# Five more slots for split operands, early splits of a down stage, and all attention units among the ups

## The chip, the cores and the metric

The kernel runs on one core of a Trainium2 chip. TensorE (PE in the profile) multiplies matrices into PSUM, VectorE (DVE), ScalarE (ACT) and GpSimd (POOL) work on tiles in SBUF and PSUM (POOL on SBUF alone), and SyncE (SP) issues the DMA transfers, in order, from one queue. The metric is the device time of one execution in microseconds.

## The reference

The reference is a banded attention followed by a gated feed-forward layer, in float32:

```
scores = q @ k^T / 8, for batch 8, 8 heads, 576 positions, head size 64
scores = where(0 <= i - j < 64, scores, -1e9)
p      = exp(scores - rowmax); p = p / (rowsum + 1e-9)
x      = (p @ v), heads side by side: 4608 tokens x 512
out    = (sigmoid(x @ w_gate) * (x @ w_val)) @ w_out      512 -> 1536 -> 512
```

The three weights arrive as float64 and are turned into float32 on the chip.

## The kernel before

**Precision.** A float32 operand that TensorE multiplies is split into a high part (a cast on ACT) and a low part (a subtraction on VectorE); a product of two operands is three matmuls, high x high, high x low and low x high (`three`). So each operand that streams through TensorE costs one ACT cast, one VectorE subtraction and a slot of 128 x 2 x 384 in SBUF.

**Stages.** Tokens are cut into 12 tiles of 384. The first two (s=0) go through a plain scheme while weights are converted. The rest go in five stages s = 1 to 5 of two tiles each. Each has an up part (the gate and value products, `product`) and a down part (the product with w_out). The up part of a stage, and the down parts from s=2 on, multiply 2 x 2 blocks with seven block products instead of eight (`PRODUCTS`, n = 0 to 6): operands are sums and differences of blocks, called B11, T1, T2, T3, T4, B21, B22, and the products are added up by `combine`. The down of s=1 is plain (`plain_down`, 24 operands in two halves each).

The ups run k = 0 to 5 (six slices of the hidden layer), and in each k the seven products n, for gate and value (m = 0, 1): 42 products of 12 matmuls. The schedule numbers them u = 7k + n. The downs from s=2 on run n = 0 to 6, and in each n the six k (`last_product`, 6 matmuls): 42 steps, called d.

**The operands.** The x operands of a stage's ups (`x_part`, `x_rest`) lie in 14 slots x0 to x13, two for each n. The operands of a down, `h_part` i = 6n + k, go into the same 14 slots in turn (`h_split`, line 702). A slot becomes free when the last k of the ups has used its x operand, so the first 14 down operands are made in the last sixth of the ups (k = 5) or just behind it, and part i > 13 when part i - 14 has been used. For T2 and T4, `rhs_of` first makes the difference on VectorE (lines 571, 573), in place of B11. Before these, `h_prep` makes T1 and T3 of a k (`differences`, lines 563 and 564), and `x_prep` does the same for x.

**PSUM.** Each of gate and value (m), or of the two halves of a down (q), has three banks, one for each sum b of the seven products (`acc[m][b]`): n = 0 and 4 go to b=0, n = 1, 3, 5 to b=1, n = 2 and 6 to b=2. Product n=3 adds onto n=1 in b=1 after VectorE has read it (`plus`, line 607), and so on; a product group waits until the readers of its bank are done. A result uses 384 of the 512 columns of a bank. Two more banks (tag a) serve attention.

**Attention units.** The attention of stage s+1 is cut into eight units (a tile and a pair of heads), run while stage s is multiplied. A unit goes through: `stage_s` (scores on TensorE, band mask and row minimum on VectorE, exponentials on ACT), `stage_n` (reciprocals of the sums on VectorE, multiplication by them on POOL, or on VectorE for s+1 = 2), `stage_b` (six transposes into PSUM, copied to pT by ACT, line 304) and the outputs pT x v. The outputs of a unit run at the start of `stage_s` of the next unit; they give three pieces of 128 columns. Two go into free columns of the two attention banks, the third into columns 384 to 511 of a bank of `acc`, found by `spare_up` (b=0, after its sum is done at n=5) or by `spare_down` (a bank of the down, taken early and marked as held). ACT copies the pieces to xf. The last unit's outputs run by themselves (`stage_c`). Exponentials and sigmoids use different tables of ACT, so each unit costs two table loads.

In the kernel before, `visit` puts a unit's scores at u = 5, 12, 19, 26, 33, 40 (units 1 to 6) and at d = 10 (unit 7); unit 0 is at u=0, or ahead of s=1. Transposes follow four products after the scores and three products before the next unit's outputs; those of unit 6 run at d=8, of unit 7 at d=18, and unit 7's outputs at d=22.

**What sets the order.** Each piece of work is put into a list with a time (`put`), the times coming from a count of TensorE's steps; the list is sorted and traced in that order. The tile framework then simulates the program and orders each engine's instructions by what is ready and by their place in the trace; TensorE's own order is kept as traced (`pe`). `tc.issue_after(ins)` holds an instruction behind `ins` in the order of `ins`'s engine, without a wait. On each engine and in SP's queue, what waits holds up all behind it.

**Weights.** `w_load` brings 512 KB of up weights for one k and n into one of seven slots W, `wo_load` 512 KB of down weights into one of seven slots wo. The first seven down weights of a stage are put 80 us ahead of its down. In the down of s=1, `wo_sums` makes the sums of w_out blocks and stores them to DRAM for later stages.

## Time and profile before

| | |
|---|---|
| three runs | 977.72, 980.62, 982.87 us; median 980.62 |
| profiled execution | 980.85 us, span of its instructions 979.0 us |
| ups of s=1, down of s=1 | 212.2 to 318.4, to 372.7 us |
| ups and down of s=2 | to 484.8, to 534.1 us |
| ups and down of s=3 | to 639.6, to 688.9 us |
| ups and down of s=4 | to 794.4, to 843.7 us |
| ups and down of s=5 | to 931.0 us, to the end |
| mean granted TensorE clock | 0.996 |

In a row of the timeline stand start, busy time, engine, line, operation, out<-in, shape and count; in square brackets the engine's idle time before the first of them and what ended it. Matmuls overlap in time, so the time that a group takes on TensorE is read from its start to the start of the next group: 12 matmuls of 384 columns show 2.2 to 2.4 us of busy time and follow each other every 2.08. Tiles: pr are up products, y down products, s and pp the two attention banks (scores, transposes), pT the transposed weights of attention; h operands of a down, wt up weights, wot down weights.

### The profile page before, as it was taken

The page shows a single profiled execution, that of the slowest core. Times are in us where ns is not written, and L with a number is a line of the kernel's source. Part 1 is how long each engine was busy: PE and PEld are TensorE (multiplying, and loading weights), DVE is VectorE, ACT ScalarE, POOL GpSimd, SP SyncE. Part 2 cuts the span into 40 slices and gives each one's busy share as a digit, 9 for nine tenths or more (in the row PEclk, how much of TensorE's full clock was granted, in tenths as well). Part 3 has the DMA queues.
Part 4 walks back from the last instruction along what each step waited for, and adds up shares of the span by engine and source line. Part 5 has one row for each costly group of instructions (what it writes and reads, how often), then busy time and mean ns, then how long its engine had stood idle before and what let it go on. Part 6 is the DMA issues. An engine that isn't in the chain of part 4 may idle for free.

```text
span 979.0 us, 20624 instructions
## 1 busy us (share of the span) xinstructions
PE 953.7 (97%) x7200; PEld 906.8 (93%) x7200; DVE 697.2 (71%) x1873; ACT 589.0 (60%) x1473; POOL 142.7 (15%) x232
## 2 busy tenths in 40 slices
PE   6899999999999998999999999999999999999998
PEld 5798999889989998999999999899999989999998
DVE  7889989656668756566877566797566697656783
ACT  7888878545757645555775555685555666412351
POOL 4201104227670000010010101010010100000000
PEclk9999999999999999899999999999999999999999
DMA  9899999948998778887779888879888876988465
GB/s 345 308 381 378 388 345 355 396 151 292 310 315 276 248 259 298 305 266 256 250 240 309 278 269 263 246 250 286 296 262 267 265 228 218 306 254 253 152 201 165
DMA packets 110839, 272.42 MB, mean 278 GB/s; under 512 B 12048, under 2 KB 42896, under 8 KB 110736
## 3 DMA queue, kind: packets, MB, share of 16 engines
q1 hardware_dynamic: 110736, 271.11, 83.0%
q8 instruction: 57, 0.93, 0.4%
q14 instruction: 46, 0.38, 0.1%
HBM read 214.17 MB, written 56.89 MB: 277 GB/s over the span
## 4 chain that ended last, share of the span: by engine, by line
PE 67%; DVE 12%; ACT 7%; DMA 5%; issue 3%; POOL 3%; SPq 1%; DVEq 0%; POOLq 0%; ACTq 0%
PE pr L597 31%; PE y L597 14%; PE ph L358 10%; PE y L414 5%; PE s L219 3%; ACT p L251 2%; DVE h L705 2%; DMA a<-w32d 2%; PE pp L299 2%; DMA wa<-w32d 2%; PE s L328 1%; POOL ws L550 1%; DVE h L571 1%; PE oo L328 1%; DVE h L640 1%
## 5 line engine op out<-in xcount | busy, mean ns | idle before, releaser
L597 PE MATMUL pr<-x_T,wt 128*128 128x384 f32 x1224 | 226.5, 336 | 4.4 <-DVE c L607 3.6
L597 PEld LDWEIGHTS pr<-x_T,wt 128*128 128x128 f32 x1224 | 211.8, 188 | 8.0 <-DVE c L607 5.9
L597 PE MATMUL pr<-x_B,wt 128*128 128x384 f32 x1008 | 189.6, 339 | 0.0
L597 PEld LDWEIGHTS pr<-x_B,wt 128*128 128x128 f32 x1008 | 176.8, 190 | 3.3 <-issue 2.9
L597 PE MATMUL y<-h,wot 128*128 128x384 f32 x1008 | 178.9, 336 | 0.3 <-DVE h L640 0.3
L597 PEld LDWEIGHTS y<-h,wot 128*128 128x128 f32 x1008 | 174.4, 188 | 1.4 <-DVE h L640 0.6
L268 POOL TENSOR_TENSOR p<-p,rs 128x384 f32<-128x384 f32 x76 | 67.1, 897 | 606.3 <-DVE rs L259 464.1
L367 ACT ACTIVATE g<-c 128x384 f32<-128x384 f32 x90 | 47.3, 525 | 129.9 <-DVE c L636 128.4
L251 ACT ACTIVATE p<-p,mn 128x128 f32<-128x128 f32 x288 | 111.1, 393 | 7.8 <-DVE mn L243 7.2
L704 ACT CAST h<-h 128x384 fp32r<-128x384 f32 x168 | 81.8, 513 | 52.1 <-PE y L597 30.8
L358 PE MATMUL ph<-x,w 128*128 128x384 f32 x576 | 106.1, 338 | 0.0
L705 DVE TENSOR_TENSOR h<-h,h 128x384 fp32r<-128x384 f32 x168 | 93.3, 584 | 17.9 <-ACT h L704 17.7
L358 PEld LDWEIGHTS ph<-x,w 128*128 128x128 f32 x576 | 99.7, 188 | 2.2 <-issue 0.9
L640 DVE TENSOR_TENSOR h<-c,g 128x384 f32<-128x384 f32 x90 | 54.9, 610 | 46.1 <-ACT g L367 40.7
L243 DVE CUSTOM_DVE_ANT_0 p<-s,m 128x128 f32<-128x128 f32 x288 | 65.6, 285 | 17.0 <-PE s L219 16.9
L304 ACT COPY pT<-pp 128x384 f32<-128x384 f32 x96 | 41.1, 481 | 36.2 <-PE pp L299 36.2
L607 DVE TENSOR_TENSOR c<-pr,p 128x384 f32<-128x384 f32 x60 | 33.1, 552 | 40.1 <-PE pr L597 40.1
L219 PE MATMUL s<-k,q 64*64 64x128 f32 x1152 | 47.3, 293 | 8.7 <-DMA k<-in_kT_dram 6.1
L367 ACT ACT_TABLE_LOAD x37 | 47.5, 1283 | 6.6 <-DMA out_dram<-yo 6.0
L251 ACT ACTIVATION_READ_ACCUMULATOR p<-p,mn 128x1 f32 x264 | 49.7, 188 | 0.0
L219 PEld LDWEIGHTS s<-k,q 64*64 64x64 f32 x1152 | 34.4, 141 | 15.5 <-DMA q<-in_qT_dram 5.0
L636 DVE TENSOR_TENSOR c<-pr,p 128x384 f32<-128x384 f32 x60 | 33.1, 555 | 20.3 <-PE pr L597 20.2
(115 smaller groups left out, 1338.3 us busy)
## 6 DMA issues: line engine op xcount, KB each, us to landing
wt<-wd SPq DMA_DIRECT2D x186, 512.0 KB, 4.5
wot<-wod SPq DMA_DIRECT2D x84, 512.0 KB, 4.5
v<-in_vN_dram SPq DMA_DIRECT2D x48, 384.0 KB, 5.1
wd<-ws SPq DMA_DIRECT2D x48, 256.0 KB, 4.9
k<-in_kT_dram SPq DMA_DIRECT2D x48, 224.0 KB, 5.0
q<-in_qT_dram SPq DMA_DIRECT2D x48, 192.0 KB, 5.0
w32d<-w SPq DMA_DIRECT2D x36, 256.0 KB, 5.4
wd<-w SPq DMA_DIRECT2D x36, 256.0 KB, 5.9
```

Of the source, the lines that this page charges most:

```text
L219: pe(nc.tensor.matmul(sc[h][half * BLK:(half + 1) * BLK, u, :], qt[h * BLK:(h + 1) * BLK, U * BLK:(U + 1) * BLK], kt[h * BLK:(h + 1) * BLK ...
L243: nc.vector.tensor_tensor_reduce(out=pt[:, u, :], in0=sc[:, u, :], in1=masks[key], op0=ALU.add, op1=ALU.min, scale=-SCALE, scalar=3.0e38, ...
L251: exp = nc.scalar.activation(pt[:, u, :], pt[:, u, :], AF.Exp, bias=mn[:, u:u + 1], scale=-1.0, **sums)
L268: eng.tensor_mul(out=pt, in0=pt, in1=rs.unsqueeze(2).broadcast_to([P, UP, P]))
L304: cp = nc.scalar.copy(pT, pp)
L358: pe(nc.tensor.matmul(ph, l, r, start=i == 0, stop=i == len(prs) - 1))
L367: act = nc.scalar.activation(g, c, AF.Sigmoid)
L414: pe(nc.tensor.matmul(yb[y], l, r, start=first and n == 0, stop=last and n == 2))
L597: pe(nc.tensor.matmul(ps, l, r, start=first and i == 0, stop=last and i == 2, skip_group_check=not check))
L640: nc.vector.tensor_mul(out=hidden(s, k)[2 * r + b], in0=c, in1=gates.pop((t, j)))
L704: nc.scalar.copy(h2[:, 0, :], src)
L705: nc.vector.tensor_sub(out=h2[:, 1, :], in0=src, in1=h2[:, 0, :].bitcast(F32))
```

## The change

- **Five slots more.** The buffer that the program reserves for DMA descriptors made on the chip shrinks to 1 KB, since every transfer here is issued by SP; in its room lie five more slots e0 to e4 of the split-operand size. `h_split` now goes around 19 slots, the five first.
- **First splits along with the ups.** For s > 1, `h_early` makes down operands 0 to 4 (n=0, k = 0 to 4) and the T2 differences of these k as soon as each k is done. Operand i is now reused for i + 19, and the due times of the other `h_part`s follow. `GUARD` holds operands 8 to 12 behind the latest `plus` on VectorE. In the plain down of s=1, the operands take the 19 slots too.
- **x operands earlier.** The slots become free earlier in a down, so `x_prep`, `x_part` and `x_rest` of the next stage are due four steps earlier (ten in the down of s=1). `x_prep` of s=2 is held behind the latest `plus`.
- **All attention units in the ups.** Scores now stand at u = 4, 9, 14, 19, 25, 30, 35 (`VISITS`), normalization at u+1, transposes at u+4, and the last outputs at u=41. So five of the six transposes that a next unit follows stand one product ahead of its outputs, and unit 0's (u=3, for s > 1) too. The third output piece goes into whichever bank fits: b=2 when n=4, b=0 otherwise, and where a sum is under way in that bank, the matmuls don't restart it. `spare_down` goes away.
- **Down weights of s=2** are due 48 us instead of 80 us ahead of their down, behind the latest `w_load` in SP's queue.

```diff
-    WB, WOB, CB = 7, 7, 3
+    WB, WOB, CB, EXTRA = 7, 7, 3, 5
...
-            oo = [sc[0][:, UP, :], sc[1][:, UP, :], spare()]
-            outputs(*done, oo)
+            piece, start = spare_up(spare)
+            oo = [sc[0][:, UP, :], sc[1][:, UP, :], piece]
+            outputs(*done, oo, (True, True, start))
...
-    def outputs(t, p, oo):
+    def outputs(t, p, oo, starts=(True,) * UP):
...
-                                    pT[h][:, U // 2, half * BLK:(half + 1) * BLK], start=True, stop=True))
+                                    pT[h][:, U // 2, half * BLK:(half + 1) * BLK],
+                                    start=starts[U // 2], stop=True, skip_group_check=not starts[U // 2]))
...
-        nc.sync.dma_start(out=w2.bitcast(F32), in_=wd[k][n])
+        marks["w_load"] = nc.sync.dma_start(out=w2.bitcast(F32), in_=wd[k][n]).ins
...
-        nc.sync.dma_start(out=w2.bitcast(F32), in_=wod[q])
+        with tc.issue_after(marks["w_load"]) if s == 2 else nullcontext():
+            nc.sync.dma_start(out=w2.bitcast(F32), in_=wod[q])
...
-        if nm == "T2":
+        if nm == "T2" and not any(src is x for x in t2_made):
...
+    t2_made = []
+    GUARD = (8, 13)
+
+    def h_early(s, k):
+        h_part(s, 0, k)
+        b11, _, _, b22, t1 = hidden(s, k)
+        nc.vector.tensor_sub(out=b11, in0=b22, in1=t1)
+        t2_made.append(hidden(s, k))
...
-        differences(nc.vector, b11, b12, b22, t1)
+        with tc.issue_after(marks["plus"]) if s == 2 else nullcontext():
+            differences(nc.vector, b11, b12, b22, t1)
...
-            nc.vector.tensor_add(out=o, in0=ps, in1=a)
+            marks["plus"] = nc.vector.tensor_add(out=o, in0=ps, in1=a).ins
...
-        h2 = xp.tile([P, 2, TT], F32R, name=f"h_{nm}", tag=f"x{i % (2 * NPR)}")
+        i %= EXTRA + 2 * NPR
+        h2 = xp.tile([P, 2, TT], F32R, name=f"h_{nm}", tag=f"e{i}" if i < EXTRA else f"x{i - EXTRA}")
...
-        hs[(s, n, k)] = h_split(f"{n}_{s}_{k}", n * NK + k, rhs_of(nc.vector, hidden(s, k), PRODUCTS[n][1]))
+        i = n * NK + k
+        with tc.issue_after(marks["plus"]) if GUARD[0] <= i < GUARD[1] else nullcontext():
+            hs[(s, n, k)] = h_split(f"{n}_{s}_{k}", i, rhs_of(nc.vector, hidden(s, k), PRODUCTS[n][1]))
...
-    def spare_up():
-        return acc[0][0][:, TT:TT + P]
-
-    def spare_down(s):
-        acc[0][2] = psum(1, 2, f"y2_0_{s}")
-        acc[0][("held", 2)] = True
-        return acc[0][2][:, TT:TT + P]
+    def spare_up(n):
+        return acc[0][2 if n == 4 else 0][:, TT:TT + P], n > 4
...
+    VISITS = (4, 9, 14, 19, 25, 30, 35)
...
-            for v in range(1, NP * 2 - 1):
-                visit(("u", NPR * v - 2), 3, *unit(s + 1, v), unit(s + 1, v - 1), spare_up)
-                visit(("u", NPR * v - 1), 4, *unit(s + 1, v))
-                visit(("u", NPR * v + 2) if v < 6 else ("d", 8), 1, *unit(s + 1, v))
-            visit(("d", 10), 3, *unit(s + 1, 7), unit(s + 1, 6), lambda s=s: spare_down(s))
-            visit(("d", 12), 4, *unit(s + 1, 7))
-            visit(("d", 18), 1, *unit(s + 1, 7))
-            visit(("d", 22), 2, *unit(s + 1, 7))
+            for v, u in enumerate(VISITS, 1):
+                visit(("u", u), 3, *unit(s + 1, v), unit(s + 1, v - 1), u % NPR)
+                visit(("u", u + 1), 4, *unit(s + 1, v))
+                visit(("u", u + 4), 1, *unit(s + 1, v))
+            visit(("u", 41), 2, *unit(s + 1, 7))
...
                 put(now + 0.5, 5, h_prep, s, k)
+                if k < EXTRA:
+                    put(now + 3, 5.1, h_early, s, k)
...
-                put(at_down[2 * i - 28] + 2.3 if i > 13 else t0 - 14.5 + 2.1 * (i // 2 + 1) if i < 10 else t0 - 1, 5.2,
-                    plain_part, i)
-            x_parts(at_down[24], lambda x: at_down[28 + 2 * x] + 2.4 if x < 10 else at_down[46] + 2.4 + 1.05 * (x - 9))
+                put(at_down[2 * i - 38] + 2.3 if i > 18 else t0 - 14.5 if i < EXTRA else t0 - 14.5 + 2.1 * ((i - 5) // 2 + 1) if i < 8
+                    else t0 - 4 if i == 8 else t0 - 0.5, 5.2, plain_part, i)
+            x_parts(at_down[14], lambda x: at_down[max(10 + 2 * x, 18 + x)] + 2.4)
...
-            if i < 12:
-                when = max(t0 - 14.5 + 2.1 * (i // 2 + 1), {5: t0 - 3.9, 11: t0 + 0.8}.get(i, t0 - 20))
+            if i < EXTRA + 2 * NPR:
+                when = max(t0 - 14.5 + 2.1 * ((i - EXTRA) // 2 + 1), t0 - 5.2 if GUARD[0] <= i < GUARD[1] else t0 - 15, {5: t0 + 0.8, 11: t0 + 0.9, 17: t0 + 1}.get(i, t0 - 20))
             else:
-                when = at_down[i - 14] + 1.2 if i > 13 else t0 + 1
-            put(when, 5.2, h_part, s, *divmod(i, NK))
+                when = at_down[i - 19] + 1.2
+            if i >= EXTRA:
+                put(when, 5.2, h_part, s, *divmod(i, NK))
             if i % 2 == 0:
-                put(at_down[i - 13] + 1.1 if i > 13 else t0 - 80 + 4 * i, 8.2, wo_load, s, i // 2)
+                put(at_down[i - 13] + 1.1 if i > 13 else t0 - 80 + 4 * i if s > 2 else t0 - 48 + 3 * i, 8.2, wo_load, s, i // 2)
         if s + 1 < NS:
-            x_parts(at_down[24], lambda x: at_down[28 + x] + 1.3)
+            x_parts(at_down[20], lambda x: at_down[24 + x] + 1.3)
...
-    nc = _bacc.Bacc("TRN2", target_bir_lowering=False, num_devices=1)
+    nc = _bacc.Bacc("TRN2", target_bir_lowering=False, num_devices=1, dynamic_dma_scratch_size=1024)
```

More of the change, by code (lines that the diff above doesn't have):

```diff
@@ L723, in plain_down @@
             at, q = (2 * b, 1)[d // 2], d % 2
-            if x == 0 and not acc[q].pop(("held", at), False):
+            if x == 0:
                 acc[q][at] = psum(1 + q, at, f"y{b}_{d}")
@@ L736, in last_product @@
             st = acc[q]
-            if n < 3 and k == 0 and not st.pop(("held", b), False):
+            if n < 3 and k == 0:
                 st[b] = psum(1 + q, b, f"y{b}_{q}_{s}")
```

## The prediction

> **What bounds the kernel now.** I read the page first, then the stretches between stage borders, then TensorE's timeline wherever a stretch is longer than its matmuls need.
>
> ```profile
> span 979.0 us, 20624 instructions
> PE 953.7 (97%) x7200; PEld 906.8 (93%) x7200; DVE 697.2 (71%) x1873; ACT 589.0 (60%) x1473; POOL 142.7 (15%) x232
> ```
>
> TensorE is the bound, so the change can only win back idle TensorE time; no matmul goes away. The next rows are the columns time, then busy time and count of PE, PEld, DVE, ACT, POOL, then clock, DMA share, GB/s. They are the ups and the down of s=4, the ups of s=5, and the last sixth of the ups of s=3.
>
> ```profile
> 688.86:794.38 105.52, 104.55 (x854) 100.11 (x853) 69.85 (x199) 59.69 (x160) 9.69 (x12) 1.00 0.83 264
> 794.38:843.65 49.27, 48.62 (x337) 47.17 (x337) 39.54 (x97) 34.51 (x86) 4.17 (x4) 1.00 0.77 245
> 843.65:931.01 87.36, 87.36 (x505) 87.36 (x505) 57.12 (x110) 24.48 (x48) 0.00 (x0) 1.00 0.73 230
> 622.74:639.58 16.84, 15.84 (x127) 14.45 (x127) 15.26 (x34) 10.39 (x24) 1.62 (x2) 1.00 0.77 239
> ```
>
> Ups without attention take 87.36 us for 504 matmuls, 173.3 ns each: no loss at all. A regular attention unit (TensorE and POOL rows of its transposes pp, its outputs and scores s; ACT's table loads and copies between):
>
> ```profile
> 410.64 0.69 PE L328 MATMUL s<-pT,v 128*64 128x64 f32 x16
> 412.30 4.45 PE L597 MATMUL pr<-x_B,wt 128*128 128x384 f32 x24
> 412.75 1.28 ACT L251 ACT_TABLE_LOAD   x1
> 416.65 1.28 ACT L367 ACT_TABLE_LOAD   x1
> 417.94 0.53 ACT L367 ACTIVATE g<-c 128x384 f32<-128x384 f32 x1
> 417.23 1.62 POOL L268 TENSOR_TENSOR p<-p,rs 128x384 f32<-128x384 f32 x2 [17.14 <-DVE rs L259]
> 420.75 0.82 PE L299 MATMUL pp<-ident,p 128*128 128x128 f32 x6
> 421.28 0.86 ACT L304 COPY pT<-pp 128x384 f32<-128x384 f32 x2 [2.06 <-PE pp L299]
> 421.33 2.33 PE L597 MATMUL pr<-x_T,wt 128*128 128x384 f32 x12
> 423.49 2.24 PE L597 MATMUL pr<-x_B,wt 128*128 128x384 f32 x12
> 427.75 0.69 PE L328 MATMUL s<-pT,v 128*64 128x64 f32 x16
> ```
>
> The period is 427.75 - 410.64 = 17.11 us, of which 84 matmuls take 14.56; a unit costs 2.55 us, all of it work. Stage s=4 lasts 105.52 + 49.27 = 154.79 us. Its matmuls need 87.36 + 252 x 0.1735 (54 of the down took 9.37, below) = 131.1, its eight units 20.4. So **3.3 us are lost** in it, and its neighbours s=2 and s=3 show the same waits at the same places. Where, for s=3 (first down matmul at 639.58), with the one row of TensorE's waits on VectorE's additions over the whole span (total, times, longest):
>
> ```profile
> PE pr L597 <- DVE c L607: 3.6, 7, 1.3
> ...
> 626.90 0.82 PE L299 MATMUL pp<-ident,p 128*128 128x128 f32 x6
> 627.92 2.35 PE L597 MATMUL pr<-x_T,wt 128*128 128x384 f32 x12 [0.20 <-DVE u L607]
> 630.11 2.25 PE L597 MATMUL pr<-x_B,wt 128*128 128x384 f32 x12
> 632.60 1.32 PE L597 MATMUL pr<-x_T,wt 128*128 128x384 f32 x6 [0.24 <-DVE c L607]
> 635.71 0.69 PE L328 MATMUL s<-pT,v 128*64 128x64 f32 x16
> 639.58 9.53 PE L597 MATMUL y<-h,wot 128*128 128x384 f32 x54
> 648.95 0.55 PE L299 MATMUL pp<-ident,p 128*128 128x128 f32 x3
> 650.35 2.36 PE L597 MATMUL y<-h,wot 128*128 128x384 f32 x12
> 652.74 1.00 PE L328 MATMUL s<-pT,v 128*64 128x64 f32 x15
> 654.78 5.49 PE L597 MATMUL y<-h,wot 128*128 128x384 f32 x30
> ```
>
> Starts against the regular durations: transposes 1.02 instead of 0.58 (0.44), the next product groups 2.49 and 3.11 instead of 2.08 (0.41, 1.03), all on VectorE's additions in `plus` (L607), which free the bank. Of the seven waits one, the longest, is in s=1 (below), and two each are here and in s=2 and s=4. In the down the transposes of unit 6 take 1.40 instead of 0.58 (0.82), the group behind 2.39 (0.3), its outputs and scores 2.04 instead of 1.66 (0.38). VectorE is busy 15.26 of 16.84 us there, and in its order T2 subtractions for splits not yet wanted stand ahead of `plus` (the third row is the reduction that each unit needs six times, with its mean of 285 ns):
>
> ```profile
> 630.59 1.49 DVE L571 TENSOR_TENSOR h<-h,h 128x384 f32<-128x384 f32 x3
> 632.00 0.55 DVE L607 TENSOR_TENSOR c<-pr,p 128x384 f32<-128x384 f32 x1
> ...
> L243 DVE CUSTOM_DVE_ANT_0 p<-s,m 128x128 f32<-128x128 f32 x288 | 65.6, 285 | 17.0 <-PE s L219 16.9
> ```
>
> **The change part by part.** The base is the profiled execution's own 980.85 us, span and 1.85 around it; the median of the runs is 980.62, so 0.23 comes off at the end.
>
> *Five slots, early splits, guard (end of the ups of s=2, 3, 4).* Five of the splits (one ACT cast, one VectorE subtraction; 1.49 for three is a step of 0.47 us with the last one's end) and five T2 subtractions move out of the last sixth of the ups into the five before it, where VectorE has room (69.85 of 105.52 us busy with the crowded last 17 in it). Against that, unit 7 moves from the down into this last sixth: six reductions, 1.7 us of VectorE, and on ACT six exponentials and two table loads, 412.75 to 417.94, 5.2 us. VectorE's need there stays near 15 us (2.3 off, 1.7 on, as many other splits as before, since 14 slots empty there as before), but the guard holds splits 8 to 12 behind the last `plus` in VectorE's order, and the matmuls need those splits only 8 us into the down. So the 1.9 us of waits on L607 should go, and with unit 6 out of the down its 1.5 us too. What is late next is ACT: 10.39 busy of 16.84 plus up to 5.2. Its exponentials feed the POOL multiplication and unit 7's transposes, four products later. Regularly that chain ends at 417.23 + 1.62 = 418.85 for transposes at 420.75: 1.9 us of slack. Kept wait: between 0 and the 3.3 of now; I take 0.6, nearer to none, because a queue of three casts (1.5 us) still fits into that slack. Gain 3 x (3.3 - 0.6) = **8.1** (0 to 9.9).
>
> *The start of s=2.* PE's rows, ACT's, SP's, and the stretch with the low clock:
>
> ```profile
> 388.95 1.00 PE L328 MATMUL s<-pT,v 128*64 128x64 f32 x15 [1.25 <-ACT pT L304]
> 391.72 1.56 PE L219 MATMUL s<-k,q 64*64 64x128 f32 x24 [1.47 <-DMA k<-in_kT_dram]
> 393.20 6.44 PE L597 MATMUL pr<-x_B,wt 128*128 128x384 f32 x24
> 386.71 1.28 ACT L367 ACT_TABLE_LOAD   x1 [5.99 <-DMA out_dram<-yo]
> 384.03 0.68 SPq L446 DMA_DIRECT2D wot<-wod  x1
> 390.79:397.61 6.82, 5.89 (x38) 5.56 (x39) 3.04 (x16) 4.87 (x18) 0.00 (x0) 0.50 1.02 415
> ```
>
> Lost: 1.25 before the outputs (ACT waited for output DMAs that hold the gate's buffer, so the pT copy was late); 2.6 in outputs and scores (388.95 to 393.20 is 4.25 instead of 1.66: the k load and half clock); 2.0 in 24 matmuls at half clock (6.44 against 4.45): 5.9 us in all, some 2.7 of it the clock (2.0, and half of the scores' 1.48). The transfers are saturated (415 GB/s), with out weights (wot, 512 KB, 1.3 us each at that rate) between; the row is the last of three. The change queues these behind the up weights and 50 us later; the three in this jam are 3.8 us. The outputs' stores go out earlier too, since the split x of s=2 starts ten part products earlier and has ACT and VectorE free by the border. Against it: the unit comes one product (2.16 us) earlier, so its outputs at 388.95 - 1.25 - 2.16 = 385.5 and its scores at 386.4, while k would land at 391.7 - 3.8 = 387.9. Bounds: no relief for k, a wait of 5.3 instead of the 2.7 of now (1.25 + 1.47), 2.6 lost; all gone, 5.9 won. With relief by three loads 1.5 stays, with earlier stores less; I take 1.1 and no half clock. Gain **4.8**. The same loads shifted into the later ups of s=2 add 3.7 MB to about 50 us, 74 GB/s on 264: below the 415 seen, and hidden by the up weights' lead.
>
> In the Trainium skill, "TensorE: Matmul & The Clock Gate", Part 1, the clock halves after an idle window of about 3.4 us and comes back after a busy one. The trace shows 6.82 us of half clock, two such windows, though TensorE was idle for only 2.7 of the 4 us before (1.25 and 1.47 in the rows); taken strictly the rule would charge this stall nothing, and 2.7 of the 4.8 would not be there to win; the measured row decides.
>
> *x_prep behind `plus` (ups of s=1).*
>
> ```profile
> 276.10 0.79 DVE L563 TENSOR_TENSOR t<-xf,xf 128x384 f32<-128x384 f32 x1 [4.04 <-POOL sw L535]
> 277.41 2.37 PE L597 MATMUL pr<-x_T,wt 128*128 128x384 f32 x12 [1.31 <-DVE c L607]
> ```
>
> VectorE stood 4 us behind a buffer that POOL held, and `plus` behind it. With x_prep of s=2 queued behind the last `plus` of these ups, this goes: gain **1.5** (0 to 1.6). One more unit, closer together, in ups where VectorE also normalizes: cost between 0 and 3 (the 1.31 above, twice); I take **0.5**.
>
> *Last down (s=5).* Its second split was late:
>
> ```profile
> 932.01 8.27 PE L597 MATMUL y<-h,wot 128*128 128x384 f32 x46 [0.31 <-DVE h L640]
> ```
>
> It is made early now: gain **0.5** (0 to 0.6, the idle 0.31 and as much again for the stream that starts anew).
>
> *One product between transposes and outputs.* The transposes of a unit now stand one product ahead of the outputs and the next scores, not three, in 23 places. pT is ready at 421.28 + 0.86 = 422.14, one product ends at 423.49: 1.35 us of slack. A gate and a table load ahead of the copy (1.28 + 0.53) would make 0.5 us of wait. The spacing puts exponentials under gates in some visits, but those end 5.6 us after the scores and the copies come at 9. Between 0 and 23 x 0.5 = 11; I take **1.0**, near none, as ACT idled 2.06 us before this copy. The third output piece now goes into a bank in use (no restart); its copy is the first that ACT makes behind the scores, and the bank's next product is one product off, 2.1 us: nothing. Without that cover the copy itself would be waited for, at most the 0.45 between scores' end (412.30) and table load (412.75) per unit.
>
> In the Trainium skill, "ScalarE: Activation LUTs", What ACT_TABLE_LOAD costs, a switch is 2.66 us, drain included; by that, ACT's block would be 2.8 us longer and the chain above would miss its transposes by 0.9 us per unit. The rows show 1.28, and the next instruction 1.29 after the load's start (416.65, 417.94), so here the drain is not there.
>
> Sum: 8.1 + 4.8 + 1.5 - 0.5 + 0.5 - 1.0 = 13.4; 980.85 - 13.4 = 967.45, less 0.23: **967.2 us**.
>
> **The rivals.**
> 1. *The start of s=2 keeps its waits.* k and the weights still jam, with the unit a product earlier, and the half clock stays: 4.8 not won, 972.0. For it: 1.5 us by my own count with all three loads gone, and stalls of 1.25 and 1.47 set the clock off. Against it: earlier stores.
> 2. *The crowd only changes engine.* ACT is full in the last sixth (10.39 + 5.2 of 16.84), its in-order queue holds casts ahead of unit 7's exponentials, POOL starts late as in the 0.82 of now, and TensorE waits there: the 8.1 falls to none, 975.3. This is also the case in which the early splits aren't made early.
> 3. *Slower: the outputs wait for pT.* Place: each of the 23 outputs one product behind its transposes. Price: with a table load and two gates ahead of the copies, 1.28 + 2 x 0.53 - 1.35 = 1.0 us each, 23 in all instead of the 1.0 in the sum: 967.2 + 22 = 989. It decides from (13.4 + 1.0)/23 = 0.63 us per visit on. For it: in the crowded down of s=3 ACT is late enough that outputs and scores take 0.38 too long. Against it: ACT's regular idle time of 2.06 before the copy.
>
> **How the numbers follow.** Forecast 0.56, rival 1 0.18, rival 2 0.15, rival 3 0.11. Range: with every loss gone, 9.9 + 5.9 + 1.6 + 0.6 = 18 off, 962.6; 962 as a round bound. Upward it takes in rivals 1 and 2: 975.7; outside lie rival 3 and small tails. Half a per cent, 4.9 us, is about what a measurement of this kernel can tell from no change. Faster (below 975.7): forecast, rival 1 and half of rival 2, 0.81. Same: the rest of rival 2 and the mild third of rival 3, 0.12. Slower 0.07.
>
> **What would show it.** Right: no wait on L607 and no 1.4 us transposes around the borders of s=2, 3, 4, stage s=4 near 152 us; no half clock near 390; VectorE not waiting for sw L535; the first down matmuls of s=5 without a gap. Wrong: PE waits on ACT pT at many outputs; on POOL p at the last unit's transposes; on k at the first visits of s=2; a new half-clock stretch.

## The result, and the profile after

| | before | after |
|---|---|---|
| median of four runs, us | 979.70 | 968.79 |
| lowest and highest, us | 977.72, 982.87 | 968.12, 970.44 |
| profiled execution, its span, us | 980.85, 979.0 | 968.12, 966.3 |
| ratio after to before | | 0.9883, 95% interval 0.9863 to 0.9902 |

The changed kernel is faster, by 1.2% (1.0 to 1.4), against 967.2 us forecast. The medians are 10.9 us apart and the profiled pair 12.7, for 13.4 forecast; the shares by stages below are those of the profiled pair.

The busy times from the page after, and the stretches of the profile (time, then busy time and count of PE, PEld, DVE, ACT and POOL, clock, DMA share, GB/s): the ups of s=2, ups and down of s=3, the ups of s=4.

```profile
PE 946.8 (98%) x7200; PEld 904.1 (94%) x7200; DVE 692.8 (72%) x1873; ACT 597.3 (62%) x1479; POOL 141.8 (15%) x232
```

```profile
372.49:481.88 109.39, 108.92 (x937) 103.97 (x937) 74.52 (x228) 74.30 (x202) 13.51 (x16) 1.00 0.91 311
...
525.67:634.45 108.78, 108.55 (x938) 103.81 (x937) 74.73 (x230) 73.75 (x200) 13.83 (x16) 1.00 0.84 268
634.45:678.24 43.79, 43.79 (x257) 43.79 (x254) 32.81 (x66) 22.75 (x47) 0.00 (x0) 1.00 0.85 276
678.24:787.47 109.23, 108.76 (x937) 103.81 (x936) 75.17 (x230) 73.76 (x200) 13.51 (x16) 1.00 0.82 261
```

As before, TensorE does 7200 matmuls and is the bound. Each down from s=2 to s=4 now takes 43.79 us for 252 matmuls, 173.8 ns each: nothing is lost in it any more, and nothing of attention is left in it. With both units that stood in the down now in the ups, 8 x 2.55 + 87.36 = 107.8 us is what the ups need; they take 1.0 to 1.6 more. Stage s=4 is 153.02 us long (before 154.79).

The end of the ups of s=3 on TensorE, the answer to the rows that the prediction shows of before:

```profile
628.66 0.82 PE L300 MATMUL pp<-ident,p 128*128 128x128 f32 x6
629.23 2.35 PE L612 MATMUL pr<-x_T,wt 128*128 128x384 f32 x12
631.42 2.25 PE L612 MATMUL pr<-x_B,wt 128*128 128x384 f32 x12
633.60 0.92 PE L329 MATMUL oo<-pT,v 128*64 128x64 f32 x24
634.45 25.75 PE L612 MATMUL y<-h,wot 128*128 128x384 f32 x147
```

Starts follow each other by 0.57, 2.19, 2.18 and 0.85: all regular. No row of TensorE's waits names `plus` (now L622). One row that they do name (total, times, longest):

```profile
PE s L329 <- ACT pT L305: 1.6, 6, 0.6
```

Of these six waits of outputs on pT, five lie in the ups of s=2 to s=4 and one in s=1. One of them, in s=3, below a regular visit of the same ups, and then the one in s=1:

```profile
548.57 2.33 PE L612 MATMUL pr<-x_T,wt 128*128 128x384 f32 x12
550.83 0.69 PE L329 MATMUL s<-pT,v 128*64 128x64 f32 x16
...
551.68 0.89 PE L219 MATMUL s<-k,q 64*64 64x128 f32 x24
...
615.68 2.33 PE L612 MATMUL pr<-x_B,wt 128*128 128x384 f32 x12
618.19 1.00 PE L329 MATMUL s<-pT,v 128*64 128x64 f32 x15 [0.18 <-ACT pT L305]
...
619.41 0.89 PE L219 MATMUL s<-k,q 64*64 64x128 f32 x24
```

```profile
251.24 1.06 PE L329 MATMUL s<-pT,v 128*64 128x64 f32 x16 [0.65 <-ACT pT L305]
...
252.80 0.89 PE L219 MATMUL s<-k,q 64*64 64x128 f32 x24
```

The product ahead of the outputs takes 2.51 us from start to start instead of 2.26, the outputs 1.22 instead of 0.85: **0.62 us lost**, in five places (two in s=2, one in s=3, two in s=4), 3.1 us in all. They are u = 14 and u = 35, where the transposes end a group of seven products. In s=1, at u = 14 too, product and outputs take 2.98 and 1.56 us, 1.4 more than regular.

The start of s=2, and the stretch around it; then the first down matmuls of s=5:

```profile
384.70 0.77 PE L329 MATMUL s<-pT,v 128*64 128x64 f32 x15
...
385.70 0.89 PE L219 MATMUL s<-k,q 64*64 64x128 f32 x24
```

```profile
384.00:390.00 6.00, 6.00 (x73) 5.51 (x72) 3.97 (x17) 5.17 (x18) 0.00 (x0) 1.00 0.99 366
```

```profile
918.62 6.69 PE L612 MATMUL y<-h,wot 128*128 128x384 f32 x36
```

Outputs and scores of s=2 start without a wait, the clock stays at 1.00, though the DMA share is still 0.99. In s=5 the first 36 matmuls stand in one row, where before a wait of 0.31 for a split cut it behind the third.

### The profile page after: what moved, and what is told of

The parts are those of the page before. It is cut to its first block, busy times and chain, and to the rows that moved or that the text cites. A ratio compares the mean times of both kernels' runs of the same rounds, so it can differ in the third digit from the quotient of the medians.

```text
span 966.3 us, 20552 instructions
## 1 busy us (share of the span) xinstructions
PE 946.8 (98%) x7200; PEld 904.1 (94%) x7200; DVE 692.8 (72%) x1873; ACT 597.3 (62%) x1479; POOL 141.8 (15%) x232
## 4 chain that ended last, share of the span: by engine, by line
PE 82%; ACT 6%; DVE 5%; DMA 3%; issue 2%; POOL 1%; SPq 0%; DVEq 0%; ACTq 0%
PE pr L612 39%; PE y L612 23%; PE ph L360 6%; PE y L416 4%; PE s L219 3%; PE pp L300 2%; PE s L329 2%; ACT p L251 2%; DMA a<-w32d 1%; DMA w32d<-w 1%; PE oo L329 1%; ACT L251 1%; ACT pT L305 1%; PE pr L329 1%; ACT L369 1%
## 5 line engine op out<-in xcount | busy, mean ns | idle before, releaser
L612 PE MATMUL pr<-x_B,wt 128*128 128x384 f32 x1008 | 187.5, 336 | 0.0
L612 PE MATMUL y<-h,wot 128*128 128x384 f32 x1008 | 176.0, 334 | 0.0
L721 DVE TENSOR_TENSOR h<-h,h 128x384 fp32r<-128x384 f32 x168 | 88.6, 553 | 24.1 <-ACT h L720 22.7
L369 ACT ACT_TABLE_LOAD x40 | 51.3, 1283 | 13.4 <-DVE c L651 12.8
L622 DVE TENSOR_TENSOR c<-pr,p 128x384 f32<-128x384 f32 x60 | 33.1, 551 | 27.7 <-PE pr L612 27.7
```

The costliest lines, as they stand in the source:

```text
L369: act = nc.scalar.activation(g, c, AF.Sigmoid)
L612: pe(nc.tensor.matmul(ps, l, r, start=first and i == 0, stop=last and i == 2, skip_group_check=not check))
L721: nc.vector.tensor_sub(out=h2[:, 1, :], in0=src, in1=h2[:, 0, :].bitcast(F32))
```

## The experiments

The time to the first up matmul of s=1 differs by 2.0 us between profiled executions (211.79 to 213.77) of kernels that are alike up to there, and s=1 itself by more than one, so the verdicts go by single stages. A stage lasts from the first matmul of its ups to that of the next one's, on TensorE's timeline; in s=2 to s=5 a stage that an edit doesn't touch repeats within 0.1 us.

| kernel | median | ratio (95%) | s=1 | s=2 | s=3 | s=4 | s=5 |
|---|---|---|---|---|---|---|---|
| before | 979.70 | 1 | 160.53 | 161.36 | 154.79 | 154.79 | 135.40 |
| after | 968.79 | 0.9883 (0.9863 to 0.9902) | 159.95 | 153.18 | 152.57 | 153.02 | 135.08 |
| e3_no_guard | 974.52 | 0.9934 (0.9914 to 0.9954) | 160.10 | 155.00 | 154.34 | 154.82 | 134.79 |
| e4_old_visits | 972.16 | 0.9914 (0.9888 to 0.9941) | 162.36 | 152.88 | 152.86 | 152.87 | 135.07 |
| e6_no_slots | 970.31 | 0.9902 (0.9871 to 0.9933) | 159.43 | 153.44 | 153.20 | 153.26 | 136.12 |
| e7_guards_alone | 975.29 | 0.9945 (0.9929 to 0.9961) | 161.79 | 155.29 | 153.89 | 153.90 | 136.12 |
| e1_wo_early | 970.45 | 0.9897 (0.9871 to 0.9923) | 159.90 | 155.03 | 152.52 | 153.03 | 135.07 |
| e8_x_late | 969.60 | 0.9892 (0.9865 to 0.9918) | 160.91 | 153.18 | 152.53 | 153.03 | 135.07 |
| e9_start_as_before | 971.19 | 0.9905 (0.9887 to 0.9923) | 160.52 | 157.31 | 152.52 | 153.03 | 135.07 |
| e2_xprep_free | 970.99 | 0.9901 (0.9877 to 0.9925) | 162.89 | 153.22 | 152.54 | 153.06 | 135.07 |
| f1_b_earlier | 969.62 | 0.9893 (0.9867 to 0.9920) | 161.52 | 152.55 | 152.98 | 152.37 | 135.07 |
| f2_split_behind_gate | 969.67 | 0.9892 (0.9872 to 0.9911) | 161.20 | 153.17 | 152.56 | 153.05 | 135.07 |
| f3_split_behind_copy | 968.68 | 0.9879 (0.9863 to 0.9896) | 160.35 | 152.98 | 152.50 | 152.83 | 135.07 |
| f4_two_splits_behind | 967.53 | 0.9880 (0.9860 to 0.9899) | 160.65 | 152.66 | 152.15 | 152.50 | 135.06 |

Each ratio is to runs of the kernel before that were taken along with it on the same chip, so two medians of the table are not to be subtracted.

### The guard taken away

```diff
-    GUARD = (8, 13)
+    GUARD = (0, 0)
```

> The changed kernel without the guard on down operands 8 to 12 (neither held behind plus nor due later). Theory: the number of VectorE operations in the last sixth of the ups hardly fell, their order is what took the waits on plus away; so waits on plus of 1 to 1.9 us return at the end of the ups of each of s=2, 3, 4 (ups 109 to 110.5 us and more), 972 to 974.5 us in all. Rival: the early splits and early T2 differences made the room; then the ups keep their length within 0.3 us, 968.8 us.

Stages s=2 to s=4 grow by 1.82, 1.77 and 1.80 us, all of it in the ups; slots, early splits and units are as in the change. TensorE's waits, then its timeline at the end of the ups of s=3:

```profile
PE pr L612 <- DVE c L622: 3.7, 6, 1.0
```

```profile
630.05 0.82 PE L300 MATMUL pp<-ident,p 128*128 128x128 f32 x6
631.07 1.32 PE L612 MATMUL pr<-x_T,wt 128*128 128x384 f32 x6 [0.20 <-DVE c L622]
633.41 1.33 PE L612 MATMUL pr<-x_T,wt 128*128 128x384 f32 x6 [1.02 <-DVE c L622]
```

These are the waits of before again, two in each of the three stages: transposes 1.02 instead of 0.57, the product behind them 3.50 instead of 2.08. With everything else of the change, s=3 and s=4 are at 154.34 and 154.82, about the 154.79 of before. The guard alone decides over these 1.8 us, as the theory had it. In s=5 it costs 0.29: without it that stage takes 134.79.

### Slots and units, each without the other

The first kernel keeps slots, early splits, guard and later weights, and puts units and x operands where they were before. The second keeps the units in the ups and the guard, without the slots and the early splits. The third has guard and later weights alone, with neither slots nor units moved. In all three the x operands are due as in the kernel before, which from s=2 on costs nothing by itself (e8 below: within 0.04 us). Without slots, the guard's line of due times also puts operand 5 some 4.7 us later than in the kernel before, so in the last two "guard" means the guard and these times.

```diff
 e4_old_visits
-            for v, u in enumerate(VISITS, 1):
+            for v in range(1, NP * 2 - 1):
...
-            x_parts(at_down[20], lambda x: at_down[24 + x] + 1.3)
+            x_parts(at_down[24], lambda x: at_down[28 + x] + 1.3)
 e6_no_slots
-    WB, WOB, CB, EXTRA = 7, 7, 3, 5
+    WB, WOB, CB, EXTRA = 7, 7, 3, 0
...
-                when = at_down[i - 19] + 1.2
+                when = at_down[i - 14] + 1.2
 e7_guards_alone: both
```

> The changed kernel with the attention units where they were before (five of seven products apart, the last two in the down, their outputs' third piece in the old banks) and, since the last unit then ends in the down, the x operands of the next stage due as before. Slots, early splits, guards and down weights of s=2 stay as changed. Theory: the downs of s=2, 3, 4 wait for unit 6 again, but less, as the split crowd is gone (0 to 1.5 us each), and the waits for pT one product behind the transposes go (1.2 us per stage): stages 151.5 to 153.5 us, 966 to 971 us in all. Rival: moving the units is what the change lives on; the ups' and downs' ends lose 3 us per stage again, 976 to 978 us.

> The changed kernel without the five slots: no early splits and no early T2 differences, down operands and x operands due as in the kernel before; attention units all in the ups, the guards and the later down weights of s=2 as changed. Theory: with unit 7 in the last sixth of the ups and five splits and five T2 differences (4.7 us of VectorE, 2.6 us of ACT) back in it, VectorE no longer gets through: the ends of the ups of s=2, 3, 4 or the first steps of their downs lose 2 to 4 us each, stages 155 to 157 us, 975 to 981 us in all, and the down of s=5 waits for its second operand again. Rival: the guard's order is enough and the slots bring nothing: stages 153 +- 0.5 us, 969 us.

> The kernel before with only the guards (down operands 8 to 12 and x_prep of s=2 behind plus) and the later down weights of s=2; no slots, no early splits, attention units and x operands where they were. Theory: the waits on plus (1.9 us per stage) go, those for unit 6 in the down (1.5 us) stay: stages of s=3 and s=4 152.9 to 153.5 us, s=2 157 us (outputs' stores still late, but no jam of down weights), s=1 159 to 160 us, 972 to 975 us in all: most of the change's gain without slots. Rival: guarded splits without early ones come too late for the down, whose first operands wait 1 to 3 us: stages 154.5 us or more, 977 us or more.

Mean of s=3 and s=4: before 154.79; guard alone 153.90; guard and units 153.23; guard and slots 152.87; all three 152.80; slots and units without the guard 154.58. So beside the guard the slots are worth 1.03 and the units 0.67, but together only 1.10: **they cure the same loss**. The down of s=3 on TensorE's timeline, with the guard alone, and with guard and units:

```profile
633.65 9.53 PE L611 MATMUL y<-h,wot 128*128 128x384 f32 x54
643.92 0.55 PE L299 MATMUL pp<-ident,p 128*128 128x128 f32 x3 [0.75 <-POOL p L268]
```

```profile
632.72 12.25 PE L612 MATMUL y<-h,wot 128*128 128x384 f32 x67
645.85 32.34 PE L612 MATMUL y<-h,wot 128*128 128x384 f32 x185 [0.88 <-DVE h L721]
678.03 2.25 PE L612 MATMUL pr<-x_B,wt 128*128 128x384 f32 x12
```

With the guard alone, no matmul of this down waits for a split (54 of them show the same 9.53 us as before), but unit 6's transposes wait for POOL longer than before: they start 10.27 us into the down instead of 9.37. With the slots this wait is gone (e4: its transposes start 9.37 us into the down, without a wait), and with the units gone from the down it is gone too: that is the loss that both cure. In e6 a split is late instead, 0.88 us, and the down takes 678.03 - 632.72 = 45.31. Only the slots take that away: 43.79. But e6 has shorter ups: 108.10, 107.89 and 107.93 us against the 109.39, 108.78 and 109.23 of the changed kernel, for the most part because the 0.62 us at five places, 3.1, is not there. So the slots give 1.5 us in each of three downs and 1.04 in s=5 (136.12 against 135.08), 5.7 in all, and take back 3.5 in the ups: 2.2 net. That the median without slots would be 975 to 981, as one theory had it, fell: it was 970.31. The theory for the guard alone held in kind, but its stages are longer than forecast: s=3 and s=4 153.90 for 152.9 to 153.5, s=1 161.79 for 159 to 160. With old visits, s=2 to s=4 lie in the forecast range (152.88), and the median, 972.16, above it, by stage s=1.

With old visits s=1 takes 162.36, 2.4 above the changed kernel and more than its scatter. There the transposes of unit 6 stand in the down and wait for VectorE, which multiplies in this stage and itself stands 4.08 us for a load of weights (until 342.19) just ahead of that multiplication:

```profile
343.23 0.99 PE L299 MATMUL pp<-ident,p 128*128 128x128 f32 x6 [2.59 <-DVE p L268]
```

This is not the units' place alone. The kernel before has the same visits; its VectorE multiplies ahead of its own wait for that load (at 338.44), TensorE waits 0.2 us for it, and s=1 takes 160.53. Which other part of the change puts the multiplication behind the load was not tried.

### The start of s=2

```diff
 e1_wo_early (down weights of s=2 as before)
-        with tc.issue_after(marks["w_load"]) if s == 2 else nullcontext():
-            nc.sync.dma_start(out=w2.bitcast(F32), in_=wod[q])
+        nc.sync.dma_start(out=w2.bitcast(F32), in_=wod[q])
...
-  ... else t0 - 80 + 4 * i if s > 2 else t0 - 48 + 3 * i, 8.2, wo_load, s, i // 2)
+  ... else t0 - 80 + 4 * i, 8.2, wo_load, s, i // 2)
 e8_x_late (x operands due as before)
-            x_parts(at_down[14], lambda x: at_down[max(10 + 2 * x, 18 + x)] + 2.4)
+            x_parts(at_down[24], lambda x: at_down[28 + 2 * x] + 2.4 if x < 10 else at_down[46] + 2.4 + 1.05 * (x - 9))
...
-            x_parts(at_down[20], lambda x: at_down[24 + x] + 1.3)
+            x_parts(at_down[24], lambda x: at_down[28 + x] + 1.3)
 e9_start_as_before: both
```

> The changed kernel, but the first seven down weights of s=2 are due 80 us ahead of their down again and not held behind the up weights. Theory: these loads took the room of the k load at the start of s=2, so three of them (3.8 us of transfers) return ahead of it, TensorE waits for k again by 2 to 3 us around the first visits of s=2 and falls to half clock: stage s=2 153.2 + 3 to 6 us, 972 to 975 us in all. Rival: it was the earlier split of the x operands and the earlier output stores that freed this border; then nothing returns, s=2 stays within 0.5 us of 153.2, 968.8 us.

> The changed kernel with x_prep and the x operands of each next stage due as in the kernel before (four steps later, ten in the down of s=1). Theory: at the border of s=1 and s=2 the splits of x and the output copies meet again, the outputs' stores go out some 5 us later, hold the gate's buffer, and the first outputs wait for pT: s=2 153.2 + 1 to 3 us; s=3 and s=4 unchanged within 0.3 us: 970 to 972 us. Rival: the later down weights alone freed that border: s=2 within 0.3 us of 153.2, 968.8 us.

> The changed kernel with the loads of the out weights of s=2 early and the split x operands due late, both as before; the units stay in the ups. Theory: it is the empty down of s=1 that frees the start of s=2, with ScalarE and SyncE at hand for the output stores, so these two edits add up to no more than they cost alone (1.85 and 0 us in stage s=2): stage s=2 near 155 us, 970.6 us, no half clock. Rival: the edits cover for each other, and with both undone the jam of transfers is back, with the half clock: stage s=2 at 158 to 161 us, 974 to 977 us.

Stage s=2 grows by 1.85, by 0.00, and by 4.13 with both. The scores at that place, with the early weights and then with both edits, and for the second the stretch of the product behind them, with its clock:

```profile
386.88 0.89 PE L219 MATMUL s<-k,q 64*64 64x128 f32 x24 [1.76 <-DMA k<-in_kT_dram]
```

```profile
388.50 0.90 PE L219 MATMUL s<-k,q 64*64 64x128 f32 x24 [2.54 <-DMA k<-in_kT_dram]
389.33 3.87 PE L611 MATMUL pr<-x_T,wt 128*128 128x384 f32 x12
```

```profile
389.33:393.03 3.70, 3.70 (x16) 3.70 (x13) 1.91 (x13) 3.52 (x12) 0.00 (x0) 0.55 1.03 400
```

The two edits do cover for each other, as the rival had it, though not to the size it gave (158 to 161): the late x operands cost nothing as long as the weights stay behind, and 2.3 us more once k is late anyway. Of these, 0.8 is the longer wait on k, 3.70 - 2.08 = 1.6 the product at a clock of 0.55, which followed the wait of 2.54 and not the one of 1.76. The theory for the early weights alone had 3 to 6 us and half clock; it measured 1.85 and none. The one for the late x operands had 1 to 3 us and measured 0.00, as its rival said. Both edits together still leave 4.05 us of the 8.18 that s=2 won; about 3.3 of that are the guard's and the down's, as in the next stages. e1 and e9 show that the late k and the half clock behind it, which these two edits bring back, were most of the loss at this place, 4.13 us of 5.9. How much of the rest is due to the output stores alone was not tried; in e7, which has only the later weights of these edits, there is no half clock either, but ACT still waits 3.27 us for the stores (until 386.22), and the ups of s=2 are 1.4 us longer than those of s=3.

### x_prep of s=2 not held

```diff
-        with tc.issue_after(marks["plus"]) if s == 2 else nullcontext():
-            differences(nc.vector, b11, b12, b22, t1)
+        differences(nc.vector, b11, b12, b22, t1)
```

> The changed kernel, but x_prep of s=2 isn't held behind the last plus of the ups of s=1. Theory: VectorE stands some 4 us behind POOL's sw in the ups of s=1 again and plus behind it: stage s=1 160.0 + 1.5 us, 970.3 us in all. Rival: with the units at other places, or the slots free earlier, x_prep finds its buffer free: no change, 968.8 us.

VectorE's timeline at its wait for POOL, and TensorE's in the products behind it:

```profile
280.21 0.80 DVE L566 TENSOR_TENSOR t<-xf,xf 128x384 f32<-128x384 f32 x1 [2.65 <-POOL sw L538]
```

```profile
292.20 0.61 PE L611 MATMUL pr<-x_T,ws 128*128 128x384 f32 x2 [0.56 <-ACT ws L546]
293.36 0.97 PE L611 MATMUL pr<-x_T,ws 128*128 128x384 f32 x4 [0.54 <-DVE ws L548]
```

Stage s=1 is 162.89, 2.94 above the changed kernel; the other kernels that leave this stage alone are at 159.90 to 161.20, so at least 1.7 of it is the edit. VectorE stands behind POOL's buffer again (2.65 us), but no product waits for `plus`. TensorE waits 0.64 us for an addition of VectorE right behind (outputs at 282.86) and, 12 us on, 1.1 us for sums of weights; that these are late because of the stand at 280 is likely, not shown.

### The outputs that wait for pT

In the changed kernel, this stands ahead of the outputs at 618.19 in the timeline of VectorE and then of ACT; last, ACT at the same place without slots (e6):

```profile
614.99 0.56 DVE L721 TENSOR_TENSOR h<-h,h 128x384 fp32r<-128x384 f32 x1
615.47 0.55 DVE L651 TENSOR_TENSOR c<-pr,p 128x384 f32<-128x384 f32 x1
...
616.60 1.02 DVE L651 TENSOR_TENSOR c<-pr,u 128x384 f32<-128x384 f32 x2
```

```profile
617.24 0.53 ACT L369 ACTIVATE g<-c 128x384 f32<-128x384 f32 x1 [1.75 <-DVE c L651]
617.67 0.84 ACT L305 COPY pT<-pp 128x384 f32<-128x384 f32 x2
618.40 0.87 ACT L627 COPY p<-pr 128x384 f32<-128x384 f32 x2
```

```profile
615.51 0.52 ACT L369 ACTIVATE g<-c 128x384 f32<-128x384 f32 x1 [1.15 <-DVE c L651]
615.94 0.84 ACT L305 COPY pT<-pp 128x384 f32<-128x384 f32 x2
```

The transposes of this unit are done by 615.92, but ACT's copy stands behind a gate, and the gate behind additions on VectorE, among which the subtraction of an early split (614.99, L721) has slipped. ACT idles 1.75 us for the last of them; without slots 1.15, and no output waits there. First, transposes one product sooner where a visit falls on n=2; then the early splits moved, in three ways.

```diff
 f1_b_earlier
-                visit(("u", u + 4), 1, *unit(s + 1, v))
+                visit(("u", u + (3 if u % NPR == 2 else 4)), 1, *unit(s + 1, v))
 f2_split_behind_gate, f3_split_behind_copy (f2 with the gate's mark, f3 with both; marks["copy"] is set to the copy in stage_b)
-        h_part(s, 0, k)
+        with tc.issue_after(marks["gate"]), tc.issue_after(marks["copy"]):
+            h_part(s, 0, k)
 f4_two_splits_behind: as f3, for k = 1 and k = 4 alone
```

> The changed kernel with the transposes of units 2 and 6 (scores at u=9 and 30, so n=2) three products behind their scores instead of four, which leaves two products to the next outputs. Theory: of the units one product ahead it is these whose pT copy stands on ACT behind the gate of n=6, and they lose 0.35 in the group ahead of the outputs and 0.37 in the outputs; this goes, and POOL, done 6.55 us behind the scores, is late for transposes at 6.3 us by 0.2 at most: s=2, 3, 4 at 151.8 to 152.3 us, 965 to 966.5 us in all. Rival: POOL is late by 0.5 us and more at each: no gain, 968.8 us or above.

> The same split queued behind the last gate only, so that its cast (0.52 us) stands between the gate and the copy of the transposed probabilities where a unit's transposes come at the end of a group. Theory that the gate's lateness is the cause and ScalarE's order after it matters too: the gate comes 0.66 us earlier, the copy behind the cast gets back only some 0.2 of it, so of the 0.71 us per place about a third is won: near 967.7 us. Rival that only the gate's lateness matters: as with the split behind the copy, near 965.3 us. Rival that neither matters: 968.8 us.

> The changed kernel with the early split of each hidden column set queued on ScalarE behind the last gate of its own group of seven products and behind the last copy of transposed probabilities; VectorE's subtraction follows it. The order on TensorE, GpSimd and SyncE stays as it is. Theory: the early split stood between the additions that feed the last gate (in the changed kernel its subtraction at 407.80 us pushed them back by some 0.66 us and the gate to 410.05), and the copy that the outputs wait for stands behind that gate; so the five places where the outputs of the ups of s=2 to 4 started 0.34 and went on 0.37 us late lose their wait: 3.5 us less, 965.3 us, stages s=2 to s=4 near 152.0, down stages still at 43.79. Rival: the early split was not the cause, the additions are late by themselves, or the split now misses its own use; 968.8 or more, with a wait on pT in the ups as before.

> The changed kernel with only the early splits of the second and the fifth group of seven products (k=1 and k=4, the two whose last product is followed by a unit's transposes) queued behind the last gate and the last copy of transposed probabilities; the other three stay where the change puts them. Theory: with all five moved, each place won 0.43 us but the split of the third group then delayed other transposes by 0.45 once per stage; with two moved the win stays and that loss goes: stages s=2 to s=4 at 152.3, 152.1 and 152.2 instead of 153.18, 152.57 and 153.02, 2.2 us less in sum, 966.6 us, which is faster than both kernels though a median may hide so little. Rival: the 0.45 comes from the second group's split being late, not the third's, or the win is given back elsewhere; stages as in the changed kernel, 968.8 us.

**Sooner transposes** trade one wait for another: 0.63 and 0.65 won in s=2 and s=4, 0.41 lost in s=3. There POOL's product is not ready:

```profile
561.47 0.55 PE L300 MATMUL pp<-ident,p 128*128 128x128 f32 x3 [0.56 <-POOL p L268]
```

**The split behind the gate** won nothing (stages within 0.03 us): its cast now stands between gate and copy. **All five behind the copy** won 0.20, 0.07 and 0.19, not the 3.5 expected: the split of the third group now stands ahead of `plus`, and the transposes behind it are held, 1.03 us from start to start instead of 0.57 (0.67 at this place in the changed kernel):

```profile
434.10 0.55 DVE L721 TENSOR_TENSOR h<-h,h 128x384 fp32r<-128x384 f32 x1
...
435.67 0.82 PE L300 MATMUL pp<-ident,p 128*128 128x128 f32 x6
...
436.70 0.62 PE L612 MATMUL pr<-x_T,wt 128*128 128x384 f32 x2 [0.21 <-DVE u L622]
```

**Two of the five behind the copy** won 0.52, 0.42 and 0.52, 1.46 of the 2.2 expected. At the place in s=3:

```profile
614.94 2.33 PE L612 MATMUL pr<-x_B,wt 128*128 128x384 f32 x12
...
617.08 0.52 ACT L720 CAST h<-h 128x384 fp32r<-128x384 f32 x1
617.20 0.72 PE L329 MATMUL s<-pT,v 128*64 128x64 f32 x16
617.49 0.87 ACT L627 COPY p<-pr 128x384 f32<-128x384 f32 x2
...
618.03 0.31 PEld L329 LDWEIGHTS pr<-pT,v 128*64 128x64 f32 x8 [0.25 <-ACT p L627]
...
618.41 0.78 PE L219 MATMUL s<-k,q 64*64 64x128 f32 x20
```

The product ahead takes its regular 2.26, so moving the split back wins 0.25 of the 0.62; the outputs still take 1.21. Their third piece goes into the bank from which ACT first copies p (L627), and now the cast stands ahead of that copy. By its stages this kernel is 1.5 us below the changed one; by medians it is 967.53 at a ratio of 0.9880 (0.9860 to 0.9899) beside 0.9883 (0.9863 to 0.9902), which cannot be told apart. A split behind the copy of p as well was not tried.

## Why the prediction was right, and where it was not

The forecast of 967.2 us was 1.6 below the median, and the range held it. The two large terms came true, in the main by the mechanisms that it named; that the sum came so near is in part luck, since two errors of 2 to 3 us cancel. Its terms:

- **Five slots, early splits, guard: 8.1 for three stages.** No loss is left at the borders and in the downs; at 3.3 us each that is 9.9, the upper bound. The 0.6 per stage kept back for a late ACT ahead of unit 7 did not come. The 1.9 us of `plus` are the guard's, as forecast (e3: 1.8 per stage); the moved splits alone would not have won them. The 1.5 of unit 6 in the down would have gone with the slots (e4) or with the unit's move (e6). What the forecast did not see is that the guard needs the slots: without them a held split is late in the down (e6: 0.88 us; in s=5, e6 and e7: 136.12 against 135.40 before).
- **The start of s=2: 4.8.** All of the 5.9 went; k was in time, without a wait. The residual of 1.1, of which k's lateness was the reason, was too much. The grounds held in kind: with the weights early again k is 1.76 us late, and with the x operands late too the half clock is back. But the credit for the early x operands was wrong as long as the weights stay behind (e8: 0.00).
- **x_prep behind `plus`: 1.5, less 0.5 for denser units in s=1.** s=1 went from 160.53 to 159.95, 0.6 for the 1.0 forecast, within that stage's scatter. The hold itself is worth more than its term (e2: 1.7 to 2.9), so the denser ups cost more than 0.5. The profile shows 1.4 us at u = 14, where the outputs wait for pT, and 0.6 for a weight sum (ws), neither of which the ups of before have; no run takes them apart.
- **The last down: 0.5.** s=5 went from 135.40 to 135.08: 0.3. The early split wins 0.6, the upper bound, and the guard takes back 0.3 (e3: 134.79).
- **One product between transposes and outputs: -1.0.** This was the mis-sized term: it measured -3.1 in s=2 to s=4 alone, and u = 14 of s=1 adds 1.4. The step that failed is "near none, as ACT idled 2.06 us before this copy": that idle time is of a visit whose copy has no gate just ahead of it. Where the transposes end a group of seven, the last gate stands ahead of the copy in ACT's order and itself waits for VectorE. The price was put on table loads and gates, that is on ACT's busy time; what it came from is an early split, a subtraction of 0.56 us on VectorE and a cast of 0.5 on ACT, that the same change had moved there: without early splits the places in s=2 to s=4 lose nothing (e6), and with the old visits no output of these stages waits for pT (e4). Rival 3, that all 23 outputs wait 1.0 us, had the right place and not the size: in s=2 to s=4, 5 of them lose 0.62, with the one of s=1 4.5 us in all, which is 0.2 per visit, where it was to decide from 0.63 on.

Measured by stages: s=1 0.58, s=2 8.18, s=3 2.22, s=4 1.77, s=5 0.32, the part before s=1 -0.36, in sum 12.7, where 13.4 was forecast: 2.9 too little was put on the first two terms, 2.1 too little on the loss at the outputs. By the terms that is 9.9 + 5.9 + 0.6 + 0.3 - 3.1 - 0.4 = 13.2; the 0.5 us left over are largely small delays in the ups, of 0.1 each, such as transposes of 0.67 instead of 0.57 (586.98). Stage s=4, forecast near 152, is at 153.02, the two late places being the difference. Rival 1 is seen in e9, which undoes what spoke against it: s=2 loses 4.13 of the 4.8. Rival 2, a full ACT that makes unit 7's transposes late, is seen in no kernel here; e3 comes near its price (974.52 for 975.3), but by waits on `plus`.

## What to carry to other kernels

Moving work from a crowded stretch to a quiet one isn't free on engines that run in order: ask at each new place what now stands behind it and who waits for that, since one split of half a microsecond on each of two engines took back 0.6 us at five places. Judge the parts of a change together as well as one by one: slots and units cured the same loss, and early weights and late operands were harmful together where one of them cost nothing. And a guard, an edit of a few words, was worth more than the room that came with it: 1.8 us a stage, against 2.2 in all for the slots.

## What the runs showed of the hardware

One idle stretch of TensorE of 1.76 us left the clock at 1.00 (e1), one of 2.54 us was followed by a product at 0.55, 1.6 us longer than regular (e9), and two of 1.25 and 1.47 us within 4 us by 6.82 us at 0.50 (before). The row of e1, with the clock of the stretch in which its wait ends:

```profile
386.00:392.00 6.00, 5.12 (x49) 4.95 (x50) 2.66 (x15) 4.11 (x15) 0.00 (x0) 1.00 1.02 405
```

The Trainium skill, "TensorE: Matmul & The Clock Gate", Part 1, puts the fall behind an idle window of about 3.4 us, seen by a window that runs freely. The falls here came after less idle time in sum, 2.5 and 2.7 us, so the rule with its figure would have missed both. The length of a gap doesn't decide by itself either: the wait of 2.59 us in the down of s=1 of e4 (at 343.23), longer than the one of e9, left the clock at 1.00. What does decide, these runs don't show.
